# Gate per token, skip term in the accumulator, 96-column K matmuls and a re-costed planner in a fused attention and state-space kernel

## The chip, the cores and the metric

The kernel runs on one core of a Trainium2 chip. The metric is device microseconds of one execution, lower is better.

## The reference

The input x is 2048 tokens of 448 features (bfloat16). Two branches read it and a gate for each token mixes them:

```python
g = sigmoid((x * gate_w).sum(-1))                 # one number per token
q = (x @ wq) as 16 heads of 28;  k = x @ wk;  v = x @ wv   # one k and v for all heads
a = softmax(q k^T / sqrt(28)) v  @ wo             # 448 -> 448
K[d, l] = Re sum_n C[d,n] exp(dt[d] A[d,n] l) dt[d] B[d,n]   # n = 256, l = 0..2047
b = causal_conv(x[:, d], K[d]) + x * Dskip        # 448 convolutions of length 2048
out = g * a + (1 - g) * b
```

## The kernel before

Everything is one core's program, made of small operations that a planner (`Prog`) orders. Each operation names its engine, an estimated duration `ns`, what it reads and writes, a priority `pr` and sometimes a lock on a PSUM bank. `schedule()` simulates the five engines: at each step it takes the operation that can start first and, among equals, the one with the lowest `pr`. The result is a fixed order for each engine (and for the DMA queue of SP, which issues nearly all transfers); `emit()` adds semaphore waits. On the chip the order never changes, so an operation that waits holds up all that stand behind it on its engine.

*Preparation.* x is loaded (into the space of `tab`), transposed into xT in four tiles of 112 features (L486), kT and the first query projection are made, V for all tokens (`prep_gate`, L618). The gate: gate_w is copied to 128 columns (GW), four groups of four 512-column matmuls (L635) give it on every partition, ACT takes Tanh (L642), DVE makes g (`grow`, L644) and 1-g (`omg`, L647). Seeds for the state-space kernel K come from exponentials and sines (`seeds`).

*Attention.* For each of 16 groups (4 query blocks of 512 times 4 groups of 4 heads) and 16 key tiles: score matmuls into psS (L941, batches of three or two 128x512 tiles, rows tiled by 32), one ACT exponential for each batch (L951, 410 in all), value matmuls into psB (L959, columns tiled by 32). At the end of a group `norm` evicts psB times g into acc (L907), sends the denominators through DRAM and back as rdenB, and multiplies (L918, onT). `qproj` (L674 to L684) makes the queries of the group after next in psX. After each query block `outp` multiplies onT by Wo (L884) in psX, adds the skip term, which is an identity matmul (L888) of xT that `bx` scaled in place (L870), and DVE adds the sum into O (L895). The last four use psS banks.

*State space.* Channels go in 28 chunks of 16. For a chunk DVE builds tables of powers (`tables`): five doubling levels of two products and an add (L759, L762, L767), then a last level from Q to U = Q times a power (L775, L777, L782). `masters` makes the multipliers for a block of chunks by squaring (L719 to L731). `kgen` multiplies tables on PE (L797, 32 columns of weights by 64 columns: U and Q) into psX; DVE evicts K (L807), a DMA writes it to DRAM. `conv` reads K back as Toeplitz tiles T (1 MB for four channels; 3 buffers), multiplies by U, the input in blocks (L853, columns tiled by 32), DVE scales by 1-g (L861), `ytr` transposes (L831) and DVE adds into O (L838). O starts as zeros, loaded from DRAM. A new chunk enters every nb/31 batches; tables have the lowest priority, conv and kgen come after the attention. All 16 stores wait for every add into O.

psX (bank 7) is shared, under a lock, by `qproj`, `outp`, `kgen` and `ytr`.

Of the kernel before, what the change touches and what calls it, by code (L numbers as in the profile page):

```python
# [11 lines left out]
P = 128  # L12

S = 2048
# [34 lines left out]
class Op:  # L49
    __slots__ = ("i", "eng", "fn", "ns", "lat", "deps", "pr", "lock", "unlock", "slot", "ndma",  # L50
                 "count", "vc", "end", "comm", "slack")


class Prog:
    SEM_NS = 60
    DMA_NS = 2200
    SLACK = {"pe": 500.0, "dve": 300.0}

# [8 lines left out]
    def op(self, eng, fn, ns, rd=(), wr=(), pr=0, lat=60, lock=None, unlock=None, comm=None, slack=None):  # L67
# [3 lines left out]
        o.comm = comm  # L71
# [41 lines left out]
    def schedule(self):  # L113
# [17 lines left out]
        dmafree = 0.0  # L131
        done = 0
        while done < n:
# [148 lines left out]
def el(n, rate=0.96, fix=62):  # L282
    return fix + n / rate


class Kernel:
# [10 lines left out]
    def build(self):  # L297
        nc = self.nc
        with self.es:
# [7 lines left out]
            self.qproj(0, 0)  # L307
            self.seeds()
# [6 lines left out]
    def alloc(self):  # L315
# [13 lines left out]
        self.GW = sb("GW", NT * P, BF)  # L329
        self.Wb = sb("Wb", P, BF)  # L330
        self.ident = sb("ident", 136, BF)
        self.absq = sb("absq", 2 * 512, BF)
# [5 lines left out]
        self.onT = sb("onT", 8 * 512, BF)  # L338
        self.grow = sb("grow", S, BF)
        self.omg = sb("omg", S, BF)  # L340
# [4 lines left out]
        self.tab = sb("tab", 2 * 6 * 32 * HC, BF)  # L345
        self.tmp = sb("tmp", 2 * 2048, BF)
        self.NTR = 3
        self.T = sb("T", self.NTR * 4096, BF)
        self.NB = 7
        self.BC = NCH // self.NB  # L350
        self.LV = 256
        self.MC = 5 * 256 + 128
# [15 lines left out]
        self.Z = nc.dram_tensor("Z_scratch", (1024,), BF).ap()  # L368
        self.R = nc.dram_tensor("R_scratch", (16 * 4 * 512,), F32).ap()

    def consts(self):
# [9 lines left out]
        pg.op("dve", lambda e: e.tensor_scalar(V(sm, 1, 1), V(sm, 0, 1), -0.5, 0.5, ALU.mult, ALU.add),  # L381
              100, rd=["s0"], wr=["s1"])
        pg.op("dve", lambda e: e.tensor_scalar(V(sm, 2, 1), V(sm, 0, 1), 0.5, 0.5, ALU.mult, ALU.add),
              100, rd=["s0"], wr=["s2"])
# [20 lines left out]
    def loads(self):  # L405
# [10 lines left out]
        def lraw(k, eng="sp"):  # L416
            pg.dma([(self.rawv(k, DT, 0, [[NM, 4], [1, NM]]), dram(ins[self.names[k]], 0, [[NM, DT], [DT * NM, 4], [1, NM]]))],
                   (448, 512), f"raw{k}", wr=[("raw", k)], eng=eng)
        pg.dma([(wks.v(0, DT, 0, [[DH, 4], [1, DH]]), dram(ins["A_wk"], 0, [[DH, DT], [DT * DH, 4], [1, DH]]))],
               (448, 56), "wk", wr=["wks"], eng="act", pr=-4)  # L420
        pg.dma([(self.dt32.v(0, P, 0, [[1, D]]), dram(ins["B_log_dt"], 0, [[0, P], [1, D]]))], (128, 896), "ldt", wr=["dt"],
               eng="act", pr=-4)
        lraw(1, "act")
        pg.op("dve", lambda e: e.tensor_copy(self.Wk.v(0, DT, 0, [[32, 16], [1, DH]]),
                                             wks.v(0, DT, 0, [[DH, 4], [0, 4], [1, DH]])), 300, rd=["wks"], wr=["Wk", "rd"], pr=-1)
        pg.dma([(wst.v(0, DT, 0, [[D, 4], [1, D]]), dram(ins["A_wq"], 0, [[D, DT], [DT * D, 4], [1, D]]))],
               (448, 896), "wq", wr=["wqs"])
# [4 lines left out]
        pg.dma([(self.Wv.v(0, DT, 0, [[32, 4], [1, DH]]), dram(ins["A_wv"], 0, [[DH, DT], [DT * DH, 4], [1, DH]]))],  # L432
               (448, 56), "wv", wr=["Wv"])
        for k in range(2, 6):
            lraw(k)
        pg.dma([(self.smallb.v(0, DT, 0, [[1, 4]]), dram(ins["gate_w"], 0, [[1, DT], [DT, 4]])),
                (self.smallb.v(0, DT, 4, [[1, 4]]), dram(ins["B_Dskip"], 0, [[1, DT], [DT, 4]]))],
               (896, 2), "sm", wr=["smb"], slow=True)
# [6 lines left out]
        pg.dma([(self.O.v(0, P, 0, [[1024, 7], [1, 1024]]), dram(self.Z, 0, [[0, P], [0, 7], [1, 1024]]))],  # L445
               (896, 2048), "oz", rd=["pad"], wr=["O"], pr=4)
# [28 lines left out]
    def prep_x(self):  # L475
        pg = self.pg
        xst, xT = self.tab, self.xT
        for hf in range(4):
            for j in range(2):
# [3 lines left out]
                def mm(e, hf=hf, j=j, t=t, o=o):  # L483
                    for T in (2 * j, 2 * j + 1):
                        for k in range(4):
                            r = e.matmul(t.v(0, DT, o + 512 * (T % 2) + 128 * k, [[1, 128]]),  # L486
                                         xst.v(0, P, (4 * hf + k) * D + DT * T, [[1, DT]]),
# [60 lines left out]
    def seeds(self):  # L548
# [30 lines left out]
        V = lambda b, off, n: b.v(0, P, off, [[1, n]])  # L579
        for s in range(2):  # L580
            o = s * 6 * 32 * HC + 2 * 32 * HC + 31 * HC
            w = [("tab", s, 0)] + [("xst", k) for k in range(4)] + [("raw", k) for k in range(5)]
            pg.op("dve", lambda e, o=o: e.memset(V(self.tab, o, HC), 1.0), 70, wr=w, pr=1.5)
            pg.op("dve", lambda e, o=o: e.memset(V(self.tab, o + 32 * HC, HC), 0.0), 70, wr=w, pr=1.5)
# [26 lines left out]
    def prep_gate(self):  # L611
# [3 lines left out]
        def mv(e):  # L615
            for kt in range(16):
                for T in range(NT):
                    r = e.matmul(self.psB.v(0, P, 32 * kt, [[1, 28]]), xT.v(0, DT, T * S + 128 * kt, [[1, 128]]),  # L618
                                 self.Wv.v(0, DT, T * 32, [[1, 28]]), start=(T == 0), stop=(T == 3), tile_position=(0, 0))
# [4 lines left out]
              rd=[("b", 6)], wr=["va"], pr=-0.2)  # L624
        pg.op("dve", lambda e: e.tensor_copy(self.GW.v(0, DT, 0, [[P, 4], [1, P]]), self.smallb.v(0, DT, 0, [[1, 4], [0, P]])),
              400, rd=["smb", ("q", 0)], wr=["GW"], pr=1)
        pg.op("dve", lambda e: e.tensor_copy(self.small.v(0, DT, 16, [[1, 4]]), self.smallb.v(0, DT, 4, [[1, 4]])),
              70, rd=["smb", ("q", 0)], wr=["dsk"], pr=1.6)
        for qc in range(4):
            t, o = self.bank(7)  # L630
            X = ("gx", qc)

            def mg(e, qc=qc, t=t, o=o):
                for T in range(NT):
                    r = e.matmul(t.v(0, P, o, [[1, 512]]), self.GW.v(0, DT, T * P, [[1, P]]),  # L635
# [432 lines left out]
```

## Time and profile before

| what | value |
|---|---|
| time, median of 3 runs | 599.13 us (596.9 to 599.34) |
| profiled execution | 599.13 us, span 597.3 us |
| busy PE / DVE / ACT | 85% / 88% / 83% of the span |
| exponentials: first, last end | 24.57 us, about 546 us |
| granted TensorE clock, mean | 0.874 |
| DMA | 136.52 MB, mean 229 GB/s |

In a row of a group, "xcount | busy, mean ns | idle" gives the number of instructions, their busy time together, the mean duration of one, and how long the engine stood idle just before them, with what ended that. In a timeline row the first number is the start, the second the duration, and the square bracket holds the idle time before and its releaser. PEld is the weight load of TensorE, SPq the DMA issues of SP.

### The profile page before, as it was taken

To read this page: it belongs to the slowest core of one execution; us is meant where nothing else is said; L and a number is where in the kernel's file an instruction comes from. 1 tells how busy PE (TensorE), PEld (TensorE's weight loads), DVE (VectorE), ACT (ScalarE), POOL (GpSimd) and SP (SyncE) were. 2 spreads that over 40 slices of the span, in tenths; PEclk is the share of its full clock that TensorE was granted. 3 is DMA by queue.
4 is the path that set the end of the run, shared out by engine and by line. 5 is a ranking of instruction groups with operands and counts; after the bars stand their busy time and mean duration, and the time that the engine had idled before them with its cause. 6 is when DMAs were issued, how large, how long until landed. Compare 5 with 4: busy or idle time off the path is not lost.

```text
span 597.3 us, 18611 instructions
## 1 busy us (share of the span) xinstructions
PE 508.3 (85%) x8290; PEld 258.7 (43%) x8290; DVE 523.7 (88%) x1152; ACT 492.8 (83%) x431; POOL 3.7 (1%) x15
## 2 busy tenths in 40 slices
PE   6769889899999898999998899998998899997371
PEld 4412123444454353445453445454544555454250
DVE  3978999999999999999999999999999999981120
ACT  4587999998999898999999899999998889996000
POOL 2000000000000000000000000000000000000000
PEclk9755565897998997898999999999989989899685
DMA  9652325756887655468868458878884888889954
GB/s 211 138 115 73 78 67 217 264 165 238 279 310 244 208 166 217 152 221 294 309 231 302 139 212 300 300 275 278 309 287 148 274 288 292 276 273 306 358 190 140
DMA packets 42960, 136.52 MB, mean 229 GB/s; under 512 B 10572, under 2 KB 25152, under 8 KB 28544
## 3 DMA queue, kind: packets, MB, share of 16 engines
q1 hardware_dynamic: 41808, 134.97, 67.7%
q8 instruction: 65, 1.06, 0.7%
q10 hardware_dynamic: 1072, 0.37, 0.4%
q14 instruction: 15, 0.12, 0.1%
HBM read 131.32 MB, written 3.86 MB: 226 GB/s over the span
## 4 chain that ended last, share of the span: by engine, by line
DVE 57%; PE 23%; ACT 13%; DMA 5%; issue 1%; SPq 0%; ACTq 0%
ACT expT L951 12%; DVE tab L759 8%; DVE tab L767 8%; DVE tmp L762 8%; PE psS L941 7%; PE psS L853 4%; PE psB L959 4%; DVE tab L775 4%; DVE tab L782 4%; DVE tmp L777 4%; DVE mbf L731 3%; PE psX L797 2%; DVE msq L719 2%; DVE cst L861 2%; DVE mbf L729 2%; PE psX L674 1%
## 5 line engine op out<-in xcount | busy, mean ns | idle before, releaser
L951 ACT ACTIVATE expT<-psS 128x1536 bf16<-128x1536 f32 (+1 forms) x410 | 473.9, 1249 | 41.3 <-PE psS L941 22.5
L941 PE MATMUL psS<-qT,kT 29*128 29x512 bf16 x1024 | 173.0, 425 | 32.6 <-ACT expT L951 29.0
L853 PE MATMUL psS<-T,U 128*32 128x128 bf16 (+7 forms) x3584 | 152.2, 304 | 17.0 <-DMA T<-KP_scratch 14.8
L853 PEld LDWEIGHTS psS<-T,U 128*32 128x32 bf16 (+7 forms) x3584 | 112.5, 152 | 46.9 <-issue 21.6
L959 PE MATMUL psB<-expT,vaug 128*32 128x512 bf16 x1024 | 111.0, 427 | 0.4 <-ACT expT L951 0.4
L941 PEld LDWEIGHTS psS<-qT,kT 29*128 29x128 bf16 x1024 | 38.6, 92 | 128.5 <-ACT expT L951 94.9
L759 DVE TENSOR_TENSOR tab<-tab,mbf 128x512 bf16<-128x512 bf16 (+4 forms) x140 | 78.3, 562 | 0.6
L767 DVE TENSOR_TENSOR tab<-tab,tmp 128x1024 bf16<-128x1024 bf16 (+4 forms) x140 | 78.0, 562 | 0.7
L762 DVE TENSOR_TENSOR tmp<-tab,mbf 128x512 bf16<-128x512 bf16 (+4 forms) x140 | 78.4, 562 | 0.0
L797 PE MATMUL psX<-tab 128*32 128x64 bf16 x1792 | 71.9, 290 | 3.5 <-DVE tab L782 1.5
L797 PEld LDWEIGHTS psX<-tab 128*32 128x32 bf16 x1792 | 53.8, 138 | 18.3 <-issue 8.5
L959 PEld LDWEIGHTS psB<-expT,vaug 128*32 128x32 bf16 x1024 | 26.5, 95 | 68.2 <-issue 65.5
L775 DVE TENSOR_TENSOR tab<-tab,mbf 128x2048 bf16<-128x2048 bf16 x28 | 34.1, 1217 | 0.0
L782 DVE TENSOR_TENSOR tab<-tab,tmp 128x2048 bf16<-128x2048 bf16 x28 | 34.0, 1215 | 0.0
L777 DVE TENSOR_TENSOR tmp<-tab,mbf 128x2048 bf16<-128x2048 bf16 x28 | 34.0, 1216 | 0.0
L861 DVE TENSOR_TENSOR cst<-psS,omq 128x512 bf16<-128x512 f32 x28 | 19.1, 681 | 14.2 <-PE psS L853 14.2
L731 DVE TENSOR_TENSOR mbf<-mst,sgn 128x256 bf16<-128x256 f32 x70 | 29.1, 415 | 0.0
L719 DVE TENSOR_TENSOR msq<-mst 128x256 f32<-128x256 f32 x63 | 26.1, 414 | 0.0
L674 PE MATMUL psX<-xT,Wq 112*128 112x512 bf16 x64 | 20.0, 444 | 0.6 <-DVE kstg L807 0.6
L918 DVE TENSOR_TENSOR onT<-acc,rdenB 128x512 bf16<-128x512 f32 x16 | 10.9, 683 | 10.7 <-DMA rdenB<-R_scratch 10.7
L729 DVE CAST mbf<-mst 128x256 bf16<-128x256 f32 x70 | 19.9, 285 | 0.1
L722 DVE TENSOR_TENSOR mst<-msq 128x128 f32<-128x128 f32 x70 | 19.7, 281 | 0.0
(108 smaller groups left out, 280.4 us busy)
## 6 DMA issues: line engine op xcount, KB each, us to landing
T<-KP_scratch SPq DMA_DIRECT2D x112, 1024.0 KB, 6.7
rdenB<-R_scratch SPq DMA_DIRECT2D x64, 64.0 KB, 3.2
U<-in_A_x_dram SPq DMA_DIRECT2D x48, 56.0 KB, 2.2
tab<-in_A_x_dram SPq DMA_DIRECT2D x4, 448.0 KB, 8.1
O<-Z_scratch SPq DMA_DIRECT2D x1, 1792.0 KB, 13.3
KP_scratch<-kstg SPq DMA_DIRECT2D x28, 64.0 KB
out_dram<-O SPq DMA_DIRECT2D x16, 112.0 KB, 1.8
U<-Z_scratch SPq DMA_DIRECT2D x1, 896.0 KB, 7.9
```

The costliest lines, as they stand in the source:

```text
L731: pg.op("dve", lambda e, k=k, io=io, sg=sg: e.tensor_tensor(mbf.v(0, P, mo + io, [[MC, BC], [HC, 2], [1, HC]]), src3(k, 1), self.sgn.v(0, ...
L759: pg.op("dve", lambda e, d=dst3, a=src, m=m, w=w: e.tensor_tensor(d, a, mbf.v(0, P, m, [[HC, 4], [0, w], [1, HC]]), ALU.mult), el(n, 1.92) ...
L762: pg.op("dve", lambda e, a=src, m=m, w=w: e.tensor_tensor(tmp.v(0, P, so, [[w * HC, 4], [HC, w], [1, HC]]), a, mbf.v(0, P, m + 128, [[HC, ...
L767: pg.op("dve", lambda e, d=d2, t=t2: e.tensor_tensor(d, d, t, ALU.add), el(n, 1.92), rd=[("tmp", s), ("tab", s, lv + 1)], wr=[("tab", s, l ...
L775: pg.op("dve", lambda e: e.tensor_tensor(dst, src, mbf.v(0, P, m, [[HC, 2], [0, 32], [1, HC]]), ALU.mult), el(n, 1.92), rd=rk + mk, wr=[(" ...
L777: pg.op("dve", lambda e: e.tensor_tensor(tmp.v(0, P, so, [[BLK, 2], [HC, 32], [1, HC]]), src, mbf.v(0, P, m + 64, [[HC, 2], [0, 32], [1, H ...
L782: pg.op("dve", lambda e: e.tensor_tensor(d2, d2, t2, ALU.add), el(n, 1.92), rd=[("tmp", s), ("tab", s, 6)], wr=[("tab", s, 6)], pr=pr)
L797: r = e.matmul(self.psX.v(32 * g, 32, 64 * jj, [[1, 64]]), tab.v(0, P, to + (4 + comp) * BLK + o, [[HC, 32]]), tab.v(0, P, to + comp * BLK ...
L853: r = e.matmul(ps.v(32 * j, 33 - m, po + 128 * k, [[1, 128]]), self.U.v(0, P, (m - 1) * D + 4 * gi + j, [[D, 33 - m]]), self.T.v(0, P, s * ...
L941: r = e.matmul(self.psS.v(0, P, 1536 * s + 512 * k, [[1, 512]]), kT.v(32 * h, DH + 1, 128 * kt, [[1, 128]]), qT.v(32 * h, DH + 1, 512 * qs ...
L951: pg.op("act", lambda e: e.activation(expT.v(0, P, 512 * (i0 % 10), [[1, n]]), self.psS.v(0, P, 1536 * s, [[1, n]]), AF.Exp, scale=SQ), 75 ...
L959: r = e.matmul(self.psB.v(32 * h, 32, 0, [[1, 512]]), vaug.v(0, P, 32 * kt, [[1, 32]]), expT.v(0, P, 512 * ((4 * st + h) % 10), [[1, 512]] ...
```

## The change

- **Planner.** DVE operations get a latency of 105 ns and a fixed cost of 69 ns (60 and 62 before). PE operations carry a tiling mode, and a change of mode costs 107 ns in the simulation. PE durations are set anew; the query projection (one operation of 1300) becomes four of 242, the output projection (one of 1700) four of 190. This alters orders, not instructions.
- **Gate.** gate_w becomes column 28 of the V weights, so the V matmuls give it for each token (29 columns). One Tanh over 128x16; g and 1-g stay per token (`gtok`). 1-g is written to DRAM in 2-byte pieces and read back as 32 rows for `omq`. The 16 gate matmuls, four wide Tanh, `grow` and `omg` go. psB is evicted by a plain copy; g is applied where the projection is added into O.
- **Skip.** O is loaded from x and multiplied by (1-g) Dskip, 16 instructions of 448 (`skip`). All adds into O wait for them. `bx` and the 64 identity matmuls go.
- **K.** The tables are laid out in runs of four channels. The last level leaves two product planes, without their add; the K matmul streams 96 columns (both products and Q), and eviction is a reduction over pairs plus a copy.
- **Masters.** Blocks of 2, 4, 4, 4, 4, 4, 4, 2 chunks in place of seven of 4; casts without the doubled copy.
- **Buffers.** Four T buffers; onT 6, absq 1.
- **Loads.** Feature d sits on partition d // 4, so wk, wq and the gate load in contiguous rows; the transposes of x read every fourth column.

```diff
     SLACK = {"pe": 500.0, "dve": 300.0}
+    SWITCH = 107.0
...
+        if eng == "dve" and lat == 60:
+            lat = 105
...
-                free[e] = r + o.ns
+                ns = o.ns
+                if e == "pe":
+                    if o.mode != pemode:
+                        ns += self.SWITCH
+                    pemode = o.mode
+                free[e] = r + ns
...
-        self.NTR = 3
+        self.NTR = 4
...
+        sizes = [2, 4, 4, 4, 4, 4, 4, 2]
...
-        pg.dma([(self.O.v(0, P, 0, [[1024, 7], [1, 1024]]), dram(self.Z, 0, [[0, P], [0, 7], [1, 1024]]))],
-               (896, 2048), "oz", rd=["pad"], wr=["O"], pr=4)
+        pg.dma([(self.O.v(0, P, 0, [[D, 16], [1, D]]), dram(x, 0, [[D, P], [P * D, 16], [1, D]]))],
+               (2048, 896), "ox", rd=[("kT", 3)], wr=["O"], pr=4)
+    def skip(self):
+        for i in range(16):
+            ov = self.O.v(0, P, D * i, [[1, D]])
+            pg.op("dve", lambda e, ov=ov, i=i: e.scalar_tensor_tensor(ov, ov, self.gtok.v(0, P, 16 + i, [[1, 1]]),
+                                                                      self.dskb.v(0, P, 0, [[1, D]]), ALU.mult, ALU.mult),
+                  el(D), rd=["gt", "dsk", "O"], wr=[("o", i)], pr=53)
...
+        pg.op("act", lambda e: e.activation(ov, self.psB.v(0, P, 28, [[32, 16]]), AF.Tanh, scale=0.5), 150,
+              rd=[("b", 6)], wr=["gt"], pr=-0.6)
...
+        pg.dma([(dram(self.G, 0, [[1, P], [P, 16]]), self.gb.v(0, P, 0, [[1, 16]]))], (2048, 2), "gw", rd=["gb"], wr=["G"], pr=3, slow=True)
...
+        for T in range(NT):
+            pg.op("pe", lambda e, T=T: e.matmul(px, self.Wq.v(0, DT, T * 512 + g * 128, [[1, 128]]), ...), 242, ...)
...
-        pr = 50 + 4 * b
+        pr = 50 + c0 if b else 1.4
...
             pg.op("dve", lambda e, k=k, io=io, sg=sg: e.tensor_tensor(
-                mbf.v(0, P, mo + io, [[MC, BC], [HC, 2], [1, HC]]), src3(k, 1),
-                self.sgn.v(0, P, sg, [[0, BC], [1, 2], [0, HC]]), ALU.mult),
+                mbf.v(0, P, mo + io, [[MC, BC], [1, 64]]), src4(k),
+                self.sgn.v(0, P, sg, [[0, 8 * BC], [1, 2], [0, 4]]), ALU.mult),
...
-                d, a, mbf.v(0, P, m, [[HC, 4], [0, w], [1, HC]]), ALU.mult),
+                d, a, mbf.v(0, P, m, [[4, 16], [0, 2 * w], [1, 4]]), ALU.mult),
...
-        pg.op("dve", lambda e: e.tensor_tensor(d2, d2, t2, ALU.add), el(n, 1.92),
-              rd=[("tmp", s), ("tab", s, 6)], wr=[("tab", s, 6)], pr=pr)
+        pg.op("dve", lambda e: e.tensor_tensor(ua, src, mbf.v(0, P, m, [[4, 8], [0, 64], [1, 4]]), ALU.mult), ...
+        pg.op("dve", lambda e: e.tensor_tensor(ub, src, mbf.v(0, P, m + 32, [[4, 16], [0, 32], [1, 4]]), ALU.mult), ...
...
-                            tab.v(0, P, to + (4 + comp) * BLK + o, [[HC, 32]]),
-                            tab.v(0, P, to + comp * BLK + o, [[2 * BLK, 2], [HC, 32]]),
+                            tab.v(0, P, qp + 2048 + o, [[4, 32]]), tab.v(0, P, to + o, [[2048, 3], [4, 32]]),
...
-            pg.op("pe", mm, 220, rd=[("tab", s, l) for l in range(7)], wr=[X, ("kst", c % 2)], pr=3,
+            pg.op("pe", mm, 165, rd=[("tab", s, l) for l in range(8)], wr=[X, ("kst", c % 2)], pr=3, mode="c32",
...
+                return e.tensor_reduce(self.kstg.v(0, P, ks * 256, [[4, 32], [1, 4]]),
+                                       self.psX.v(0, P, 0, [[1, 32], [96, 4], [32, 2]]), AX.X, ALU.add)
...
-        pg.op("pe", mm, 1700, rd=["Wo"] + [("xq", T, qc) for T in range(4)] + [("on", (qc % 2) * 4 + g) for g in range(4)],
+        for g in range(4):
+            pg.op("pe", lambda e, g=g: e.matmul(t.v(0, P, o, [[1, D]]), self.onT.v(...), self.Wo.v(...), ...), 190, ...)
...
-            pg.op("pe", mm, 330, rd=sorted(rd, key=str), wr=bk, pr=-0.5)
+            pg.op("pe", mm, 215, rd=sorted(rd, key=str), wr=bk, pr=-0.5, mode="r32")
...
-            pg.op("pe", mm, 390, rd=["va"] + [("e", (4 * st + h) % 10) for h in range(4)], wr=[("b", 6)], pr=0,
+            pg.op("pe", mm, 225, mode="c32", rd=["va"] + [("e", (4 * st + h) % 10) for h in range(4)], wr=[("b", 6)], pr=0,
```

More of the change, by code (lines that the diff above doesn't have):

```diff
@@ L337, in alloc @@
         self.denT = sb("denT", 2 * 16, F32)
-        self.onT = sb("onT", 8 * 512, BF)
-        self.grow = sb("grow", S, BF)
-        self.omg = sb("omg", S, BF)
+        self.onT = sb("onT", 6 * 512, BF)
+        self.gtok = sb("gtok", 32, F32)
+        self.gb = sb("gb", 16, BF)
+        self.dskb = sb("dskb", D, BF)
         self.omq = sb("omq", 128, F32)
@@ L785, in kgen @@
+        pg.op("dve", lambda e: e.tensor_tensor(ub, src, mbf.v(0, P, m + 32, [[4, 16], [0, 32], [1, 4]]), ALU.mult),
+              el(2048, 1.92), rd=rk + mk, wr=[("tab", s, 7)], pr=pr)
     def kgen(self, c):
@@ L967, in main @@
         self.uload()
+        self.skip()
         self.masters(0)
```

259 lines of the change are left out of this document (116 added, 143 removed).

## The prediction

> **What bounds the kernel now.** I read the page first, then busy time by stage, the waits, and the timeline where the waits fall. The first view is the page's head and its busy line.
>
> ```profile
> span 597.3 us, 18611 instructions
> ...
> PE 508.3 (85%) x8290; PEld 258.7 (43%) x8290; DVE 523.7 (88%) x1152; ACT 492.8 (83%) x431; POOL 3.7 (1%) x15
> ```
>
> Three engines are near full, so an average cannot say which one sets the pace. The stages can: each row is a window, then busy us of PE, PEld, DVE, ACT, POOL, then granted clock, DMA share and GB/s.
>
> ```profile
> 30.00:100.00 70.00, 58.13 (x398) 14.65 (x402) 61.79 (x162) 61.45 (x56) 0.00 (x0) 0.55 0.41 116
> 30.00:546.00 516.00, 466.35 (x7649) 229.41 (x7649) 495.92 (x1097) 478.20 (x416) 0.00 (x0) 0.89 0.69 231
> 100.00:515.00 415.00, 379.30 (x6700) 198.89 (x6692) 411.66 (x901) 387.98 (x337) 0.00 (x0) 0.95 0.72 247
> 530.00:545.00 15.00, 14.19 (x290) 7.98 (x281) 7.83 (x10) 14.92 (x15) 0.00 (x0) 1.00 0.94 314
> 546.00:598.00 52.00, 21.88 (x448) 15.39 (x436) 7.46 (x13) 0.61 (x2) 0.00 (x0) 0.69 0.66 229
> ```
>
> From 100 to 515 us DVE is busy 411.66 of 415: it paces that stage. ACT idles 27.0 us there, PE 35.7. From 530 to 545 the tables are nearly done, DVE is half idle, and ACT idles 0.08 of 15: the exponentials run without a gap once DVE lets them. After 546 us no exponential is left, yet 51.3 us pass. So there are two targets: DVE work in the middle, and the tail. The exponentials and what they wait for in 100 to 515:
>
> ```profile
> L951 ACT ACTIVATE expT<-psS 128x1536 bf16<-128x1536 f32 (+1 forms) x410 | 473.9, 1249 | 41.3 <-PE psS L941 22.5
> ACT expT L951 <- PE psB L959: 15.1, 28, 1.6
> ACT expT L951 <- PE psS L941: 10.6, 25, 1.2
> ```
>
> PE is named, but PE is itself held up. One case from the timeline:
>
> ```profile
> 333.91 0.93 PE L884 MATMUL psX<-Wo,onT 128*128 128x448 bf16 x4 [1.05 <-DVE O L895]
> ...
> 335.95 2.37 ACT L951 ACTIVATE expT<-psS 128x1536 bf16<-128x1536 f32 x2 [1.46 <-PE psB L959]
> ```
>
> The output projection waits 1.05 us for DVE to empty psX, the next score and value matmuls stand behind it in PE's fixed order, and the exponential starts 1.46 us late. The tail:
>
> ```profile
> 534.66 1.22 DVE L782 TENSOR_TENSOR tab<-tab,tmp 128x2048 bf16<-128x2048 bf16 x1
> ...
> 546.66 0.40 PE L959 MATMUL psB<-expT,vaug 128*32 128x512 bf16 x4 [0.40 <-ACT expT L951]
> ...
> 552.72 0.25 DVE L914 RECIPROCAL denT<-denT 128x16 f32<-128x16 f32 x1 [4.91 <-DMA denT<-acc]
> ...
> 566.67 0.69 DVE L918 TENSOR_TENSOR onT<-acc,rdenB 128x512 bf16<-128x512 f32 x1 [10.67 <-DMA rdenB<-R_scratch]
> ...
> 584.35 1.21 PE L853 MATMUL psS<-T,U 128*32 128x128 bf16 x32 [2.23 <-DMA T<-KP_scratch]
> ...
> 587.49 7.92 SPq L103 DMA_DIRECT2D out_dram<-O  x16
> ```
>
> The last table add ends at 535.9. The last denominators need 20 us through DRAM, among T loads; four output projections stand on PE in front of the rest of the convolution, which then waits for T loads until 585.
>
> **The change part by part: DVE.** Rows by form (busy, mean ns), and two timeline rows for the pitch:
>
> ```profile
> L782 DVE TENSOR_TENSOR tab<-tab,tmp 128x2048 bf16<-128x2048 bf16 x28 | 34.0, 1215 | 0.0
> L731 DVE TENSOR_TENSOR mbf<-mst,sgn 128x256 bf16<-128x256 f32 x70 | 29.1, 415 | 0.0
> L729 DVE CAST mbf<-mst 128x256 bf16<-128x256 f32 x70 | 19.9, 285 | 0.1
> L722 DVE TENSOR_TENSOR mst<-msq 128x128 f32<-128x128 f32 x70 | 19.7, 281 | 0.0
> L759 DVE TENSOR_TENSOR tab<-tab,mbf 128x512 bf16<-128x512 bf16 x28 | 11.7, 418 | 0.2
> L807 DVE CAST kstg<-psX 128x256 bf16<-128x256 f32 x28 | 11.7, 417 | 3.0 <-PE psX L797 2.9
> L870 DVE SCALAR_TENSOR_TENSOR xT<-xT,small,omg 112x512 bf16<-112x512 bf16 x16 | 11.3, 747 | 0.0
> L918 DVE TENSOR_TENSOR onT<-acc,rdenB 128x512 bf16<-128x512 f32 x16 | 10.9, 683 | 10.7 <-DMA rdenB<-R_scratch 10.7
> L759 DVE TENSOR_TENSOR tab<-tab,mbf 128x128 bf16<-128x128 bf16 x28 | 6.1, 216 | 0.0
> L644 DVE TENSOR_SCALAR grow<-omg,small 128x512 bf16<-128x512 bf16 x4 | 1.6, 412 | 3.3 <-ACT omg L642 3.3
> 518.74 1.21 DVE L775 TENSOR_TENSOR tab<-tab,mbf 128x2048 bf16<-128x2048 bf16 x1
> 519.88 1.22 DVE L777 TENSOR_TENSOR tmp<-tab,mbf 128x2048 bf16<-128x2048 bf16 x1
> ```
>
> A row lasts 1.22 but the next starts after 1.14, so I count each instruction at its mean less 0.08.
> - The last table add goes: 28 x 1.14 = -31.9.
> - In its place each chunk's K is evicted in two: a reduction over 256 inputs (as L807, no change) and a copy of 128, at L722's pitch 0.20: 28 x 0.20 = +5.6.
> - Sixteen 512-wide skip products (0.67) become sixteen 448-wide ones (by width 0.59): -1.3. They move from the middle to before the first add into O, ahead of the second chunk's tables.
> - Gate: four L644 (0.33), four complements and the weight copy go, four tiny ones come: about -2.5.
> - Masters: 66 full and 22 half-size casts at about 0.14 and 0.10 instead of 77 at 0.20: -4.0; the other instructions of the eighth block, 30 squarings and products and 11 sign products more of smaller size, +2.5.
> - Copying psB without the gate, and evicting the projection with it, are the same widths: 0.
> - Table operands now come in runs of four elements. No row shows such a run at the double rate. Bounds: 0, or the single rate (rivals). I take 0, since the present rows hold one rate however often a mask row of 32 is repeated (216, 418 and 1215 ns for 128, 512 and 2048 elements lie on one line).
> Sum: -31.6 us of DVE, 27 to 29 of it after 100 us.
>
> **PE, ACT, DMA.**
>
> ```profile
> 43.21 1.82 PE psX L635 x4
> L797 PE MATMUL psX<-tab 128*32 128x64 bf16 x1792 | 71.9, 290 | 3.5 <-DVE tab L782 1.5 <-DVE qT L684 1.1 <-DVE O L838 0.5
> L853 PE MATMUL psS<-T,U 128*32 128x128 bf16 (+7 forms) x3584 | 152.2, 304 | 17.0 <-DMA T<-KP_scratch 14.8
> L888 PE MATMUL psX<-ident,xT 112*128 112x112 bf16 x48 | 4.3, 212 | 0.0
> 404.35 0.39 PE L941 MATMUL psS<-qT,kT 29*128 29x512 bf16 x2
> 404.67 0.40 PE L959 MATMUL psB<-expT,vaug 128*32 128x512 bf16 x4
> 404.89 1.02 PE L853 MATMUL psS<-T,U 128*32 128x128 bf16 x28
> T<-KP_scratch SPq DMA_DIRECT2D x112, 1024.0 KB, 6.7
> rdenB<-R_scratch SPq DMA_DIRECT2D x64, 64.0 KB, 3.2
> smallb<-in_B_Dskip_dram SPq DMA_DIRECT2D x1, 0.9 KB, 5.3
> ```
>
> - Gate matmuls: four groups of 1.82 leave PE between 36 and 49 us, at half clock, where ACT runs from hand to mouth, together with four wide Tanh. I count -4 on the exponentials' start, of at most 7.3. If something else starves ACT there, 0.
> - 96-column K matmuls: busy time for each is 40.1 ns with 64 columns and 42.5 with 128, so 96 cost +1.2 ns x 1792 = +2. Upper bound by columns alone: 71.9 x 0.5 = +36; the 128-column row speaks against it.
> - Skip matmuls gone: -4.3 in the loop, about -2 in the tail.
> - Mode switches: a score group is followed 0.32 us later by the value group (two tilings), the value group 0.22 later by the convolution (one tiling). A switch costs 0.10. The planner's old 330, 390 and 1700 ns become about these values. Splitting the query and output projections lets score matmuls in between: bound 16 x 6 x 0.10 = +10 on PE, against 35.7 idle; I take +3, hidden.
> - The gate now goes out in 2048 two-byte pieces and comes back. A 448-piece load takes 5.3 us; between that and 2048/448 x 5.3 = 24 us, starting no later than the old gate's end (43.21 + 1.82), it is back before the first convolution result needs it, which stands behind the first chunk's tables, K and T loads. Behind it on SP stand the U loads; it has low priority, so 0 taken, up to +5 if it delays them.
> - O is loaded from x instead of zeros: the same 1.8 MB, 0.
> - Fourth T buffer: a slot is held for 6.7 us of landing, some 3 of convolution and 2 of issue, 11.7 us. Three slots give a load each 3.9 us, four each 2.9. This only matters where the convolution is behind, in the tail.
>
> **The sum.** ACT's end: 546 less 4 (start) less 18 of the 27.0 idle us. I take two thirds because DVE stays nearly full until the tables end, while the stalls behind the output projection shrink; the bounds are 0, and 37.8 for all idle time from 30 us (516 - 478.2). So 524. The tables end near 536 - 32 - 3 = 501, more than 20 us ahead of ACT (now 10), so the four T loads of the last chunk can land by about 525 and the convolution is over before the last norm. The tail is then 1.5 for values and copy, 9 for two DRAM hops, 4.5 for the third (3.2 plus issue), 1 for the reciprocal and product, 4 x 1.1 + 0.6 for the projections, 9.8 for the stores (587.49 to 597.3): 31. End 555. The profiled execution took 599.13, 1.83 outside its span, and equals the median of the runs. Predicted: 557.
>
> **The rivals.**
> - *The tail stays.* The fixed PE order again puts the last projections ahead of the convolution, or T loads again slow the denominators. For it: 584.35 shows both at once. Against: 20 us of lead and the fourth slot. 524 + 51.3 + 1.8 = 577.
> - *The exponentials stay tied to DVE's order.* For it: the 1.05 us wait above is DVE's, and DVE stays full until 501. Against: the planner's shorter costs change what stands behind such waits. ACT then keeps its 27.0/415 of idle time until the tables end and gains it only over the 32 us by which they end sooner: 4 + 2. It ends at 540, the time is 540 + 30 + 1.8 = 572.
> - *The sign product reads more slowly.* Its constant now changes every four elements instead of every 32. From 415 up to L918's 683 for twice the elements: 66 x 0.27 + 22 x 0.13 = +20.6 of DVE, two thirds of the saving: 557 + 12 = 569. [...]
> - *The other side: short runs lose the double rate.* 3 x 3968 + 2 x 2048 = 16,000 elements a chunk, (683 - 418)/512 = 0.52 ns each: +8.3 us a chunk, +232 in all, about 790. It decides once 14% of that is lost, which eats the 32 us. For it: no row has such runs. Against: the element type and unit steps are unchanged.
> - *No effect.* PE is 91% busy in the stage, and could hold ACT where DVE did: 599.
>
> **Chances.** Forecast (542 to 566) 0.52; better 0.08; tail stays 0.15; tied to DVE 0.08; sign 0.05; no effect 0.04; slower 0.08. The range 538 (ACT without idle time, 508 + 31 - 1) to 588 (half the ACT gain and the old tail: 546 - 11 + 51.3 + 1.8) leaves out less than 0.2. Faster than 0.5%, about what a measurement of this kernel can tell from no change: 0.88.
>
> **What would show it.** L759 to L777 with the same means and no L782; L731's mean at 415; DVE's share in the middle below 97%; exponentials ending near 524; T waits after them under 3 us. Table means above 1.3 us for 2048 elements, or convolution matmuls after the last projection, would make it wrong.

## The result and the profile after

The changed kernel takes 580.28 us (median of 4 runs, 579.36 to 581.73) against 599.24 for the kernel before: ratio 0.9684, 95% interval 0.9637 to 0.9731. Forecast were 557 and a gain of 42; the gain is 19. The time lies inside the range of 538 to 588. Two single runs of the experiments below were over 1.5% slower than the fastest run of their kernel, and are left out of its median and ratio.

The head of the page of after, then its busy time by stage (window, then PE, PEld, DVE, ACT, POOL, clock, DMA share, GB/s):

```profile
span 578.8 us, 18479 instructions
...
PE 491.5 (85%) x8210; PEld 243.9 (42%) x8210; DVE 494.6 (85%) x1197; ACT 488.9 (84%) x428; POOL 3.7 (1%) x15
```

```profile
30.00:100.00 70.00, 47.23 (x329) 10.89 (x329) 53.82 (x178) 53.13 (x47) 0.00 (x0) 0.55 0.44 82
100.00:515.00 415.00, 386.42 (x6893) 195.07 (x6894) 401.10 (x949) 397.82 (x346) 0.00 (x0) 0.94 0.74 261
```

DVE gave up 29.1 us of work, as forecast (31.6), and in the middle ACT idles 17.2 us instead of 27.0. But from 30 to 100 us all engines do less than before: ACT 53.13 instead of 61.45. The timeline there, SP's issues and then the two waits on PE and ACT:

```profile
36.74 0.38 SPq L106 DMA_DIRECT2D G_scratch<-gb  x1
39.64 0.67 SPq L106 DMA_DIRECT2D U<-Z_scratch  x1
53.38 0.32 SPq L106 DMA_DIRECT2D kstg<-G_scratch  x1
54.90 22.35 SPq L106 DMA_DIRECT2D U<-in_A_x_dram  x32
77.29 0.68 SPq L106 DMA_DIRECT2D denT<-acc  x1
78.75 10.90 SPq L106 DMA_DIRECT2D U<-in_A_x_dram  x16
89.69 0.59 SPq L106 DMA_DIRECT2D KP_scratch<-kstg  x1
...
98.41 1.22 PE L864 MATMUL psS<-T,U 128*32 128x128 bf16 x32 [11.24 <-DMA T<-KP_scratch]
...
100.22 2.36 ACT L948 ACTIVATE expT<-psS 128x1536 bf16<-128x1536 f32 x2 [11.62 <-PE psS L938]
```

Read it from the bottom. The exponentials stop for 11.62 us because the score matmuls stand behind the first convolution on PE; that one waits 11.24 us for its T load; the T load waits for the first K write, which SP issues at 89.69, after 48 issues of U; and U starts at 54.90. Two things hold U until then: SP stands at the gate's read back (kstg<-G) until 53.38, and the zero fill of U (U<-Z, issued at 39.64) lands only 15.2 us later, behind the 2048 two-byte pieces of the gate.

The kernel before had no such wait, though its first K write goes out almost as late. First before, then the same eviction of K after:

```profile
85.67 0.42 DVE L807 CAST kstg<-psX 128x256 bf16<-128x256 f32 x1 [0.18 <-PE psX L797]
86.68 0.60 SPq L103 DMA_DIRECT2D KP_scratch<-kstg  x1
...
100.05 0.69 PE L853 MATMUL psS<-T,U 128*32 128x128 bf16 x16
```

```profile
71.92 0.28 DVE L818 CAST kstg<-psX 128x128 bf16<-128x128 f32 x1
```

Before, the first K was ready at 86.1 us, when all of U had been issued, and the first convolution stood late enough on PE to wait for nothing. After, K is ready at 72.2, 14 us earlier, and its write stands 17.5 us behind U's issues on SP, while PE comes to the convolution at 87.2 (98.41 - 11.24). Which part of the change brings K forward (the first block of masters is half as large, the gate's wide operations are gone) was not tried by itself.

The tail, after the last exponential at 516.33 + 20.28 = 536.6 (the tables end at 523.3):

```profile
516.33 20.28 ACT L948 ACTIVATE expT<-psS 128x1536 bf16<-128x1536 f32 x18 [0.54 <-PE psB L956]
522.10 1.16 DVE L788 TENSOR_TENSOR tab<-tab,mbf 128x2048 bf16<-128x2048 bf16 x1
...
543.28 1.22 PE L864 MATMUL psS<-T,U 128*32 128x128 bf16 x32 [1.75 <-DMA T<-KP_scratch]
...
543.51 0.25 DVE L911 RECIPROCAL denT<-denT 128x16 f32<-128x16 f32 x1 [2.16 <-DMA denT<-acc]
...
559.81 0.36 PE L864 MATMUL psS<-T,U 128*32 128x128 bf16 x4 [1.52 <-DMA T<-KP_scratch]
560.50 0.69 DVE L915 TENSOR_TENSOR onT<-acc,rdenB 128x512 bf16<-128x512 f32 x1 [8.53 <-DMA rdenB<-R_scratch]
561.25 5.05 PE L885 MATMUL psS<-Wo,onT 128*128 128x448 bf16 x16 [1.09 <-DVE onT L915]
566.24 1.08 PE L864 MATMUL psS<-T,U 128*30 128x128 bf16 x28
...
569.05 7.91 SPq L106 DMA_DIRECT2D out_dram<-O  x16
```

42.2 us pass instead of the forecast 31. PE walks from T load to T load until 560 (32 convolution matmuls, a wait, the next 32); the denominators' last hop is issued on SP among them; the last 28 convolution matmuls stand behind the projection, which the prediction named as a sign that it is wrong.

### The profile page after: what moved, and what is told of

It reads as the page before. It is cut to its first block, busy times and chain, and to the rows that moved or that the text cites. A ratio compares the mean times of both kernels' runs of the same rounds, so it can differ in the third digit from the quotient of the medians.

```text
span 578.8 us, 18479 instructions
## 1 busy us (share of the span) xinstructions
PE 491.5 (85%) x8210; PEld 243.9 (42%) x8210; DVE 494.6 (85%) x1197; ACT 488.9 (84%) x428; POOL 3.7 (1%) x15
## 4 chain that ended last, share of the span: by engine, by line
PE 44%; ACT 36%; DMA 9%; DVE 4%; SPq 4%; issue 1%; ACTq 0%
ACT expT L948 35%; PE psS L938 13%; PE psS L864 12%; PE psB L956 8%; PE psX L803 5%; SPq L106 4%; DMA U<-Z_scratch 3%; PE psX L885 2%; PE psX L678 2%; DMA R_scratch<-denT 1%; DMA denT<-acc 1%; PE psS L510 1%; DMA rdenB<-R_scratch 1%; DMA T<-KP_scratch 1%; DVE O L466 1%
## 5 line engine op out<-in xcount | busy, mean ns | idle before, releaser
L948 ACT ACTIVATE expT<-psS 128x1536 bf16<-128x1536 f32 (+1 forms) x410 | 472.1, 1253 | 34.8 <-PE psS L938 19.6
L864 PEld LDWEIGHTS psS<-T,U 128*32 128x32 bf16 (+7 forms) x3584 | 114.7, 151 | 56.8 <-issue 27.4
L769 DVE TENSOR_TENSOR tab<-tab,mbf 128x128 bf16<-128x128 bf16 (+4 forms) x140 | 78.9, 566 | 0.4
L778 DVE TENSOR_TENSOR tab<-tab,tmp 128x128 bf16<-128x128 bf16 (+4 forms) x140 | 78.5, 566 | 0.4
L772 DVE TENSOR_TENSOR tmp<-tab,mbf 128x128 bf16<-128x128 bf16 (+4 forms) x140 | 78.4, 563 | 0.0
L803 PE MATMUL psX<-tab 128*32 128x96 bf16 x1792 | 58.9, 268 | 2.7 <-issue 2.1
L803 PEld LDWEIGHTS psX<-tab 128*32 128x32 bf16 x1792 | 43.5, 116 | 14.9 <-issue 8.4
L786 DVE TENSOR_TENSOR tab<-tab,mbf 128x2048 bf16<-128x2048 bf16 x28 | 34.1, 1219 | 0.0
L788 DVE TENSOR_TENSOR tab<-tab,mbf 128x2048 bf16<-128x2048 bf16 x28 | 34.0, 1212 | 0.0
L740 DVE TENSOR_TENSOR mbf<-mst,sgn 128x256 bf16<-128x256 f32 (+1 forms) x80 | 30.7, 383 | 0.0
L728 DVE TENSOR_TENSOR msq<-mst 128x256 f32<-128x256 f32 (+1 forms) x72 | 27.6, 383 | 0.0
L915 DVE TENSOR_TENSOR onT<-acc,rdenB 128x512 bf16<-128x512 f32 x16 | 10.9, 684 | 13.9 <-DMA rdenB<-R_scratch 13.9
L731 DVE TENSOR_TENSOR mst<-msq 128x128 f32<-128x128 f32 (+1 forms) x80 | 21.3, 266 | 0.0
L904 DVE COPY acc<-psB 128x512 f32<-128x512 f32 x16 | 11.0, 688 | 10.3 <-PE psB L956 10.3
L734 DVE SCALAR_TENSOR_TENSOR mst<-mst 128x128 f32<-128x128 f32 (+1 forms) x72 | 19.2, 267 | 0.0
## 6 DMA issues: line engine op xcount, KB each, us to landing
U<-Z_scratch SPq DMA_DIRECT2D x1, 896.0 KB, 15.2
```

The costliest lines, as they stand in the source:

```text
L740: pg.op("dve", lambda e, k=k, io=io, sg=sg: e.tensor_tensor(mbf.v(0, P, mo + io, [[MC, BC], [1, 64]]), src4(k), self.sgn.v(0, P, sg, [[0, ...
L769: pg.op("dve", lambda e, d=dst, a=src, m=m, w=w: e.tensor_tensor(d, a, mbf.v(0, P, m, [[4, 16], [0, 2 * w], [1, 4]]), ALU.mult), el(n, 1.9 ...
L772: pg.op("dve", lambda e, a=src, m=m, w=w: e.tensor_tensor(tmp.v(0, P, so, [[4 * w, 32], [1, 4 * w]]), a, mbf.v(0, P, m + 64, [[4, 32], [0, ...
L778: pg.op("dve", lambda e, d=d2, t=t2: e.tensor_tensor(d, d, t, ALU.add), el(n, 1.92), rd=[("tmp", s), ("tab", s, lv + 1)], wr=[("tab", s, l ...
L786: pg.op("dve", lambda e: e.tensor_tensor(ua, src, mbf.v(0, P, m, [[4, 8], [0, 64], [1, 4]]), ALU.mult), el(2048, 1.92), rd=rk + mk, wr=[(" ...
L788: pg.op("dve", lambda e: e.tensor_tensor(ub, src, mbf.v(0, P, m + 32, [[4, 16], [0, 32], [1, 4]]), ALU.mult), el(2048, 1.92), rd=rk + mk, ...
```

## The experiments

In the table, the first K write is SP's issue time, the wait is the longest of a convolution on a T load before 120 us, the tail is from the last exponential's end to the end of the span. Times are medians; the rest is from each kernel's profile. The granted clock of single runs lies between 0.87 and 0.91, and in most kernels the time goes with it (e6b: 574.83 us at 0.889, 582.88 at 0.866; e9: 582.0 at 0.897, 584.08 at 0.889; not in e6: 591.88 at 0.874, 594.01 at 0.887), so differences under some 4 us are left open unless intervals part.

| kernel | us | ratio to before, 95% | first K write | wait | last exponential | tail |
|---|---|---|---|---|---|---|
| before | 599.2 | | 86.7 | none | 546.6 | 50.7 |
| after | 580.3 | 0.964 to 0.973 | 89.7 | 11.2 | 536.6 | 42.2 |
| e1, 32-byte gate write | 571.8 | 0.947 to 0.960 | 84.4 | 5.4 | 526.5 | 41.8 |
| e2, planner told | 566.2 | 0.937 to 0.949 | 74.9 | none | 521.1 | 43.0 |
| e3, gate on chip | 572.6 | 0.948 to 0.960 | 83.2 | 8.3 | 528.8 | 44.0 |
| e13, U not behind zero fill | 562.9 | 0.934 to 0.945 | 80.7 | 2.2 | 520.7 | 40.2 |
| e11, that and 3 issues | 559.3 | 0.931 to 0.940 | 74.5 | none | 520.4 | 39.3 |
| e12, before with e11's U | 595.5 | 0.991 to 0.996 | 85.8 | none | 550.6 | 43.6 |

**The early wait.** The theory: the two-byte write holds SP and the DMA engines. The rival: 48 issues on SP are slow in any case. e1 changes only the shape of the write (the right order of the tokens in 1-g is left out):

```diff
-dram(self.G, 0, [[1, P], [P, 16]]), ... (2048, 2)
+dram(self.G, 0, [[16, P], [1, 16]]), ... (same planned cost)
```

> The DRAM write of 1-g goes out as 128 contiguous pieces of 32 bytes instead of 2048 of 2 bytes; same number of issues, same order on every queue (the read back then finds the tokens in another order: the order of the tokens in the convolution's factor 1-g is left out). Theory A (the early 11.6 us wait of the first convolution comes from the two-byte write: it holds SP and the DMA engines, the U loads and the first KP write go out some 13 us late): the U loads are all issued by about 78 us instead of 89.65, the wait T<-KP_scratch of 11.2 us at 98 us falls under 2 us, time 580.3 - 11 = 569 (567 to 572). Rival B (48 U issues of 0.64 us each on SP are late whatever the write costs): the first KP write still after 86 us, time 577 to 581.

e3 has no gate transfer at all (a transpose and four small matmuls make `omq`):

> 1-g reaches its layout without DRAM: TensorE transposes the 128x16 tile, DVE copies it, four 64-column matmuls with the anti-diagonal weights; both gate DMAs are gone. Theory A: as e1, 567 to 571, the first KP write by about 76 us, no wait of more than 2 us on T<-KP_scratch before 120 us. Rival B: 577 to 581.

e2 keeps all transfers and only tells the planner what they cost:

```diff
-        pg.dma([... self.gb ...], (2048, 2), "gw", ..., slow=True)
+        pg.dma([... self.gb ...], (2048, 2), "gw", ..., slow=True, ns=15000)
-                free[e] = r + 450.0 * o.ndma
+                free[e] = r + 640.0 * o.ndma
```

> Same transfers as the changed kernel, the two-byte write included; only the planner is told 15 us for that write and 0.64 us for each issue, so it writes out another order for all engines. Theory A: the wait moves off TensorE's path because the order no longer puts the first convolution ahead of attention work: 569 to 575, wait T<-KP_scratch under 4 us in all. Rival C (the transfer itself takes the DMA engines and the lost 12 us return wherever the order puts them): 577 to 583.

SP's timeline in e1:

```profile
41.22 0.67 SPq L106 DMA_DIRECT2D U<-Z_scratch  x1
41.94 0.61 SPq L106 DMA_DIRECT2D kstg<-G_scratch  x1
49.33 22.43 SPq L106 DMA_DIRECT2D U<-in_A_x_dram  x32
71.80 0.68 SPq L106 DMA_DIRECT2D denT<-acc  x1
73.24 11.08 SPq L106 DMA_DIRECT2D U<-in_A_x_dram  x16
84.36 0.59 SPq L106 DMA_DIRECT2D KP_scratch<-kstg  x1
...
93.36 1.23 PE L864 MATMUL psS<-T,U 128*32 128x128 bf16 x32 [5.40 <-DMA T<-KP_scratch]
```

Each theory is half right. The read back no longer waits and the time falls by 8.5, at the edge of the expectation, but 5.4 us of wait stay. What is left is visible: U still starts only when the zero fill has landed (41.22 to 49.33), then takes 34 us of issues. e3 misses its expectation on all three figures: with no gate transfer at all the first K write goes out at 83.2, 8.3 us of wait stay, and 7.7 us are gained. So the gate's transfers are some 8 us of it, and not the whole. e2 gains 14.1, more than it was expected to, with the two-byte write in place: its order puts the first K write between two parts of U and no convolution on PE before 111.8, 24 us after the issue of its first T loads (87.77); no convolution waits for a T load before the tail. So what counts is whether PE comes to the first convolution before its T does, more than the bandwidth that the gate takes.

e13 and e11 are meant to take the two remaining suspects apart. e13 gives the U rows keys of their own, so they don't wait for the zero fill, which writes other parts of U; e11 also makes 3 issues of 48:

```diff
-            pg.dma(lst, (1024, 896), f"u{k}", rd=["sw"], wr=["U"], pr=2)
+            pg.dma(lst, (1024, 896), f"u{k}", rd=["sw"], wr=[("U", k)], pr=2)        # e13, e11
+                     dram(x, 64 * blk * D, [[D, 64], [-64 * D, 16], [1, D]])         # e11: one of three
```

> Changed kernel with the two-byte gate write kept; the 48 issues of U rows become three of 16 blocks each (the blocks in descending order by a negative stride, same bytes and descriptors), no longer ordered behind the zero fill. Theory A2 (after the run with the 32-byte pieces the first KP write still went out at 84.36 us: the larger part of the early wait is SP's 34 us for 48 issues): U is issued by about 58 us, the first KP write by 76 us, no wait of over 2 us on T<-KP_scratch before 120 us, 566 to 571. Rival A1 (the two-byte write is the whole of it and would hold SP and the DMA engines here too): wait of 5 us or more, 575 to 580.

> Changed kernel, U still in 48 issues, but no longer ordered behind the zero fill of U (they write other parts of it). Tells the two parts of the run with three issues apart. Theory A3 (the wait for the zero fill, which lands 15 us after its issue behind the two-byte pieces, is the part that matters): U issues start near 41 us and end near 76, the first KP write goes out by 78, 559 to 563. Theory A4 (48 issues of 0.64 us are too many in any case): first KP write after 80 us, a wait of 3 us or more on T<-KP_scratch, 567 to 573.

e13, SP and PE, then e11, SP and its stages:

```profile
41.90 16.26 SPq L106 DMA_DIRECT2D U<-in_A_x_dram  x16
...
58.83 21.09 SPq L106 DMA_DIRECT2D U<-in_A_x_dram  x32
...
80.70 0.59 SPq L106 DMA_DIRECT2D KP_scratch<-kstg  x1
...
89.48 0.84 PE L864 MATMUL psS<-T,U 128*32 128x128 bf16 x20 [2.23 <-DMA T<-KP_scratch]
```

```profile
41.25 15.80 SPq L106 DMA_DIRECT2D U<-in_A_x_dram  x3
57.09 2.87 SPq L106 DMA_DIRECT2D kstg<-G_scratch  x1
...
74.45 0.58 SPq L106 DMA_DIRECT2D KP_scratch<-kstg  x1
...
30.00:100.00 70.00, 56.09 (x474) 15.53 (x474) 61.42 (x189) 63.03 (x57) 0.00 (x0) 0.63 0.51 119
100.00:515.00 415.00, 386.85 (x7100) 200.06 (x7100) 401.06 (x953) 402.87 (x352) 0.00 (x0) 0.96 0.76 269
```

e13 gains 17.3 us; the K write at 80.70 is later than its theory said, the time is as it said. It cuts more than one link: with the order behind the zero fill gone, the planner also puts 16 issues of U ahead of the gate's read back, on which SP stood until 53.38 in after, and arranges the rest anew. Of the 15.9 us by which its exponentials end sooner, 7.2 lie between 30 and 100 us (ACT 60.29 for 53.13) and 8.4 in the middle (406.20 for 397.82, at a clock of 0.98 for 0.94). So the early wait is worth some 7 to 9 us of it, and what the rest is worth without the clock is not shown. The 48 issues add 3.6 more, with intervals that overlap. e11 fell below its expectation, 559.3 for 566 to 571. Of its 16.2 us on the last exponential, 9.9 lie between 30 and 100 us (ACT 63.03 for 53.13), the wait itself; 5.1 lie in the middle. There the clock is 0.96 for 0.94, and two other kernels with the order of after (e10, e6b; clock 0.96 in both) had ACT at 400.54 and 401.34 us in this stage, so some 3 of the 5 may be the clock's; this is not settled. The skip products, the load of O from x and the two-byte write are all still in e11, so none of them alone is what holds ACT early.

Would the kernel before gain as much from U in three issues?

> The kernel before, with U in three issues as above and nothing else changed. Theory K (before, DVE set the pace and the first convolution waited for nothing, so the U issues cost nothing there): 594 to 600, and the change on top of it is worth 35 to 40 us, about the forecast 42. Rival (three issues are worth as much in the kernel before): 577 to 584, and the change on top of it is worth about 20.

It gains 4.4 us (0.9934, 0.9908 to 0.9960). With the same U loads in both, the change is worth 595.5 - 559.3 = 36 us.

**Is DVE still the pace?** One run adds a table add of 2048 per chunk on DVE (+32 us), one cuts a table product from 2048 to 128 elements (-27 us):

> Changed kernel with one more 2048-element table add per chunk on DVE (28 x 1.14 = 32 us, the work that the change removed; its result is used by nobody). Theory F (DVE is no longer the pace by itself: 14 us idle in 100 to 515 us and the early wait absorb part): plus 10 to 20, 590 to 600. Rival G (DVE is still the pace at 96.7% of the middle): plus 27 to 32, 607 to 612.

> Changed kernel in the same order, the second top-level table product cut from 2048 to 128 elements from chunk 2 on (26 x 1.05 = 27 us less on DVE; most of that half of the table keeps an older chunk's values, so half of the long-lag part of the convolution is left out). Theory F: TensorE and ACT now set the pace, minus 0 to 6, 574 to 580. Rival G: minus 18 to 27, 553 to 562.

593.5 (0.9887 to 0.9951 of before) and 581.6 (0.9645 to 0.9767): plus 13 and plus 1. The second run keeps the order of after: 27 us less on DVE, and no gain (theory F had 574 to 580). The first is planned anew, and there the exponentials end before the tables:

```profile
527.13 1.94 ACT L950 ACTIVATE expT<-psS 128x1536 bf16<-128x1536 f32 x2 [0.31 <-PE psB L958]
...
547.58 1.22 DVE L788 TENSOR_TENSOR tab<-tab,mbf 128x2048 bf16<-128x2048 bf16 x1
```

With 32 us more on DVE the exponentials end at 529.1, 7.5 us sooner than in after; what grows is the tail (64.5). So in after DVE no longer paces the exponentials. It sets when the tables end, and that only counts where it comes last. This refutes the rival of exponentials tied to DVE, and my account of the saving with it: I had the tables end 35 us earlier; they ended 12.6 earlier (535.9 to 523.3).

**TensorE's share and the planner's costs.** K matmuls with 128 columns in the order of after (0.9701 to 0.9801 of before), and the planner with its old costs (0.9784 to 0.9874):

> Changed kernel in the same order, K matmuls with 128 columns instead of 96, at the new stride of 8 bytes in the table (the fourth 32-column block is computed and not read). Columns theory: the K matmuls go back from 58.9 to about 72 us, as before the change. Stride theory (the 64-byte stride made them slow before): they stay near 59 to 63 us. For the time: if TensorE and ACT set the pace (theory F) 13 us more on TensorE give 583 to 592; else 579 to 582.

> Changed kernel, but the planner with the costs of before (no 107 ns for a change of TensorE's mode, 60 ns of latency and 62 ns of fixed time on DVE), so only the order differs. Theory H (the modelled switches pack TensorE's order): more changes of mode, PE busy plus 3 to 8 us, 583 to 592. Rival: the order alone is worth nothing that can be told, 577 to 583.

12.5 us more of K matmuls cost 2.7 us (582.95), with intervals that overlap: TensorE isn't the only pace either. The old costs cost 7.5 us (587.77), as theory H's range had it, but not by its mechanism: PE busy is 486.4, not more. ACT waits for score matmuls 39 times (27.4 us) instead of 18 (19.6), and the exponentials end at 549.1.

**The tail.** Is it T loads, the denominators' hops, or PE's order? First, the last 12 T loads are halved:

```diff
+        w = 4096 if gi < 100 else 2048
-        pg.dma([(self.T.v(0, P, s * 4096, [[1, 4096]]), ...
+        pg.dma([(self.T.v(0, P, s * 4096, [[1, w]]), ...
```

> Changed kernel, but the last 12 of 112 T loads (chunks 25 to 27) move 4 KB per partition instead of 8 KB; order and counts unchanged (the second half of these T tiles keeps the values of an earlier chunk, that part of the last 48 channels is left out). Theory D (the tail of 42.2 us is bound by T loads at 2.75 us each): about ten loads behind the last exponential save 1.3 us each, the next limit is the denominator chain and the last projection: 566 to 570, tail 29 to 32 us. Rival E (the tail is bound by the denominator's hops through SP, or by TensorE's own convolution matmuls): 577 to 580, tail 39 us or more.

571.75 (0.948 to 0.9587), tail 34.7 for 42.2: T loads are 7.5 of the 11.2 us by which the tail exceeds its forecast, less than I said. The next limit appears at 548.82, where the last product waits 5.5 us for rdenB:

```profile
546.16 1.22 PE L865 MATMUL psS<-T,U 128*32 128x128 bf16 x32 [1.00 <-DMA T<-KP_scratch]
548.12 0.35 PE L865 MATMUL psS<-T,U 128*32 128x128 bf16 x4 [0.74 <-DMA T<-KP_scratch]
548.82 0.69 DVE L916 TENSOR_TENSOR onT<-acc,rdenB 128x512 bf16<-128x512 f32 x1 [5.50 <-DMA rdenB<-R_scratch]
```

Three T buffers in place of four:

> Changed kernel with three T buffers instead of four (the planner orders anew). Theory D (the tail is bound by T loads, which a fourth buffer lets follow one another at 2.75 us instead of 3.9): 10 loads x 1 us, 586 to 591. Rival: the fourth buffer is worth nothing here, 578 to 582.

582.8 (0.9706 to 0.9806): plus 2.5, between the two expectations. The tail is 48.9, 6.7 longer, but in this order the exponentials end 5.9 earlier.

Then on top of e11: K matmuls ahead of the convolution's and 2.75 us for a T load in the planner, throughout (b2) or from chunk 22 on (b4); the last denominators' transfers on ACT's queue (b5); the gate on the chip (b3, b6, b7).

```diff
-wr=[X, ("kst", c % 2)], pr=3, mode="c32"            ... wr=[("T", s)], pr=1, ns=3300)
+wr=[X, ("kst", c % 2)], pr=3 if c < 22 else 2.2 ... ... wr=[("T", s)], pr=1, ns=3300 if gi < 88 else 2750)
```

> The kernel with U in three issues (559.3 us, tail 39.3 us), and the planner told 2.75 us for a T load instead of 3.3 and to put the K matmuls ahead of the convolution's when both are ready. Theory D2 (T loads before the end follow at 3.9 us because TensorE's order holds their buffers; the loads of the last two chunks, 2.75 us each, are what is left at the last exponential): seven or eight loads left become five or six, tail 32 to 35 us, 551 to 556. Rival: the order of the K matmuls moves no load, tail 38 us or more, 557 to 562.

> U in three issues; the planner puts K matmuls first and counts 2.75 us for a T load from chunk 22 on only, so the order up to there stays that of the 559.3 us run. Theory D2: last exponential at 520 to 523, tail 32 to 35, 553 to 558. Rival (what the tail gains, the exponentials lose again, as in the run with this order throughout): 559 to 563.

> As the run before in this call, and the three transfers of the last group's denominators issued on ACT's queue instead of SP's. Theory E2 (with fewer T loads left the denominators' hops, behind T issues on SP, end the tail): rdenB lands 3 to 5 us earlier, 2 to 4 us less than the run before. Rival (the last projection stands behind the last convolution in TensorE's order, which waits for T loads): the same within 1.5 us.

| kernel | us | ratio, 95% | last exponential | tail |
|---|---|---|---|---|
| b2, throughout | 562.1 | 0.935 to 0.944 | 528.1 | 32.2 |
| b4, from chunk 22 | 555.4 | 0.923 to 0.933 | 518.8 | 34.5 |
| b5, and ACT's queue | 557.7 | 0.927 to 0.937 | 519.8 | 35.2 |
| b3, as b2, gate on chip | 561.7 | 0.935 to 0.945 | 526.2 | 33.3 |
| b6, as b5, gate on chip | 555.5 | 0.922 to 0.930 | 516.7 | 35.6 |
| b7, as b4, gate on chip | 556.0 | 0.927 to 0.930 | 519.2 | 35.1 |

b2 does what its theory says to the tail and the middle takes it back: the exponentials end 7.7 us later than in e11. b4 keeps most of both; against e11 its interval still overlaps. b5 is no faster than b4, so leaving SP's queue brings nothing that can be told. First b4, then b5:

```profile
527.77 0.25 DVE L906 RECIPROCAL denT<-denT 128x16 f32<-128x16 f32 x1 [3.46 <-DMA denT<-acc]
```

```profile
518.49 7.76 SPq L106 DMA_DIRECT2D T<-KP_scratch  x4
...
521.75 1.12 ACTq L106 DMA_DIRECT2D denT<-acc  x1
...
534.11 0.25 DVE L908 RECIPROCAL denT<-denT 128x16 f32<-128x16 f32 x1 [7.67 <-DMA denT<-acc]
```

On ACT's queue denT is issued at once and lands 12 us later, among four T loads; on SP's queue the planner put it ahead of two of them (519.98 to 527.77, 8 us). What the gate on the chip does once U is in order (b3 stands against b2, b6 against b5, b7 against b6):

> As the run before in this call, and 1-g transposed on the chip instead of through DRAM. If the two-byte write still costs something once the 48 issues are gone (in the run with three issues the read back of G waited at 57 us, the first KP write at 74.45 us did not): 1 to 3 us less than the run before. If not: the same within 2 us.

> As the run before in this call, and 1-g transposed on the chip instead of through DRAM, with no gate transfer left on SP. If the two-byte write is covered now, the same within 2 us; if not, 2 to 5 us less.

> The best run so far (555.5 us) with the last denominators back on SP's queue. On ACT's queue denT<-acc landed some 13 us after the last values matmul, since four T loads were issued ahead of it at once; on SP's queue it went out between them and landed in 8. If that is all: 2 to 4 us less, 551 to 554; if the last T load sets the end in both: the same within 1.5 us.

Nothing or 2 us; b6 and b7 can't be told apart, so no effect of the queue of the last denominators is shown. Both beat the two kernels of this case: 0.926 and 0.929 of before, for 0.968 of after.

## Why the prediction was wrong, step by step

The span was forecast at 555 and measured at 578.8. Of the 23.8 us between them 12.6 lie on the last exponential and 11.2 in the tail.

- *DVE's sum* (-31.6): measured -29.1. The rates held:

```profile
L786 DVE TENSOR_TENSOR tab<-tab,mbf 128x2048 bf16<-128x2048 bf16 x28 | 34.1, 1219 | 0.0
L788 DVE TENSOR_TENSOR tab<-tab,mbf 128x2048 bf16<-128x2048 bf16 x28 | 34.0, 1212 | 0.0
L740 DVE TENSOR_TENSOR mbf<-mst,sgn 128x256 bf16<-128x256 f32 x60 | 25.0, 416 | 0.0
```

  Runs of four elements keep the rate (1215 before), so the rival of 790 us is out. The sign product takes 416 for 415, so that rival (569) is out too: a constant that changes every four elements (416) reads no slower here than one that changes every 32 (415).
- *The gate write, "0 taken, up to +5 if it delays the U loads": the step that failed.* The transfer's own length was bounded well (36.74 to 53.38, 17 us, for 5.3 to 24). Wrong was the price of the delay. I named the U loads behind it and did not follow them: the zero fill behind the write, U behind the zero fill, the K write behind 48 issues, the first convolution behind that, and the attention's matmuls behind the convolution on PE. In the place of 0 to 5 us, ACT stood still for 11.62. The gate is only a part of it: without its transfers 8.3 us of PE's wait stay (e3). The rest is that the first K is ready 14 us earlier than before, so that U's issues, behind which no K stood before, now stand in front of it; my sum counted the smaller first block of masters as DVE work alone. With U out of the way no wait is left (e11), and the time is 21.0 us lower, though a part of that lies in the middle and stays open.
- *Gate matmuls, 4 us on the exponentials' start*: right in direction, and larger, though which part of the change does it was not tried by itself. By 50 us ACT has done 18.4 us of exponentials for 12.2 before; by 100 us the wait has eaten it (53.4 for 56.5), in e11 it is still there (62.4).
- *ACT's end, 524*: 536.6 with the wait, 520.4 without it (e11). ACT idles 12.1 us in the middle there, 14.9 less than before, for 18 forecast. The reason I gave, DVE's idle time, doesn't hold in after (e6, e6b).
- *The tail, 31: mis-sized, 42.2, and 39.3 in e11.* "The convolution is over before the last norm" fails. The tables do not run 23 us ahead of ACT but 13 (13.9 in e11), since DVE was no longer short. And a T load is not issued as soon as the last K is written: in after the last K write goes out at 530.08, the last three T loads from 544.54 on, each once a convolution has left a buffer. So seven T loads (e11) are left, 2.8 us each, and the denominators' hops go out among them: in after the DMA share is 1.00 from 536.6 to 550 us, and DVE waits 2.16 us for denT and 8.53 for rdenB.
- *Rival "the tail stays", 577*: near the measured time by accident. Its shape came true in part (T loads, convolution behind the projection), its 51.3 us did not.
- *96-column K matmuls, +2*: -13.0 us of busy time (71.9 to 58.9), worth a few us of time at most, as 12.5 more cost 2.7 (e9). *Fourth buffer, in the tail alone*: right, 6.7 us of tail, 2.5 of time (e4). *Mode switches, hidden*: not tested apart from the order, which is worth 7.5 (e5).

The range's lower end, 538, leaves out the 1.8 us outside the span that the forecast counts; with them it is 541, and nothing hangs on it. With the early wait gone the sum closes: 520.4 + 39.3 = 559.7 of span, for 524 + 31 = 555 forecast, 3.6 better on the exponentials, 8.3 worse in the tail.

## What to carry to other kernels

When a transfer is put ahead of others on an ordered queue, follow every link behind it, write-after-write orders between parts of one buffer included, to the engine where it comes out: here a 4 KB write and 48 issues of U stopped an engine that reads neither for 11.6 us. And when a change makes a result ready earlier, look at what stands in front of its way out: it may have stood there unnoticed before. A planner can only hide what its costs show; telling it two truer prices gave back 14.1 us (e2) without touching a transfer. And once an engine stops being the pace, work taken off it no longer brings its followers forward one for one.

## What the runs showed of the hardware

- 2048 pieces of two bytes took 17 us from their issue to the read back (after, 36.74 to 53.38), and a 0.9 MB fill behind them landed after 15.2 us, 8.1 in e1 with 128 pieces of 32 bytes.
- An issue of 64 rows of 896 bytes held SP 0.73 us (35.02 for 48 in e3); three issues for the same rows took 9.66 in b7, where no gate write stood ahead.
- K matmuls, busy time for each: 40.1 ns with 64 columns before, 32.9 with 96 after, in another order, 39.8 with 128 in e9, in the order of after. First after, then e9:

```profile
L803 PE MATMUL psX<-tab 128*32 128x96 bf16 x1792 | 58.9, 268 | 2.7 <-issue 2.1 <-DVE O L849 0.5
```

```profile
L803 PE MATMUL psX<-tab 128*32 128x128 bf16 x1792 | 71.4, 296 | 0.7 <-DVE O L849 0.5 <-issue 0.2
```

  At the new stride of 8 bytes 32 columns more cost 6.9 ns, so 64 would cost an estimated 26. The 71.4 us are what the columns theory of e9 expected, but that theory was wrong to count 128 columns for the kernel before: it had 64, at a stride of 64 bytes and 14 ns dearer than this line. The stride is the likely reason; it was not tried by itself.
